# Memory reads of an attention kernel: twelve full-array products, or three blocks of sixteen 32x32 tiles in the score banks

## The chip, the cores and the metric

The kernel runs on one core of a Trainium2 chip. The metric is the device time of one execution in microseconds. Five engines work side by side, each on its own list of instructions in order: PE (TensorE, matmuls; its weight loads are shown as PEld), DVE (VectorE), ACT (ScalarE), POOL (GpSimd) and SP, which here only issues DMAs. They wait for each other through semaphores. Matmuls write PSUM, eight banks of 128 partitions by 512 float32 values; VectorE and ScalarE read the banks.

## The reference, cut to what matters

```python
g = sigmoid((x * gate_w).sum(-1))            # x: 2048 x 448, 16 heads of 28
for s in range(4):                           # segments of 512 rows
    p = softmax(qs @ ks.T * scale + mask); a_dot = p @ vs
    pq = phi(qs)                             # t + 1 if t > 0 else exp(t)
    a_mem = (pq @ M) / (pq @ z + 1e-6)       # M: 28 x 28 and z: 28, for each head
    outs.append(gb * a_mem + (1 - gb) * a_dot)   # gb = sigmoid(beta), one for each head
    M = M + phi(ks).T @ vs;  z = z + phi(ks).sum(0)
a = concat(outs) @ wo
b = (gelu(layernorm(x).T @ w1 + b1) @ w2 + b2).T  # w1: 2048 x 1792, w2: 1792 x 2048
out = g * a + (1 - g) * b
```

In the first segment M and z are zero, so there is nothing to read from the memory.

## The kernel before, in words

The kernel is a list of operations, made once by Python, each with the engine it runs on, what it reads and writes, and a name. `ORDER` (line 286 on) then gives for each engine the order of the names as a fixed list: an engine never runs ahead of its list. Waits follow from what operations read and write. In the PE list `name@4` says that the operation takes PSUM bank 4 (of the four rotating banks 4 to 7), and `u1-3*2` stands for u1-3 and u1-4.

The names that matter:

- `lo…`, `pr…`: projections of x to queries, keys and values (`pair`, line 654). `tk`, `gk`, `gq` are DMAs on SP: transposes of the key features, and a regrouping of the last four heads through DRAM.
- `sc{p}_{f}` (`scores`, line 930): the scores of two units at a time. A unit is one segment and a group of four heads; u = 4 s + group, sixteen in all. One operation fills banks 0 to 3, four row tiles of 28 rows at once (line 942), and `exp{p}_{f}` on ScalarE reads all four banks in one instruction of 128 x 2048 (line 951). There are 40 of them, five for two units, and they share these four banks. Masks (line 954) are GpSimd's.
- `pv{u}` (line 978): probabilities times values, four column strips of 32.
- `mem{u}` (line 965, from unit 4 on): the read of the memory, one product of 512 columns. The four heads' M lie in one 128 x 128 matrix with zeros off the diagonal (`mst_sb`). The result goes to a rotating bank.
- `ta{u}` (line 994) and `tm{u}` (line 992): VectorE's transposing copies of the two results out of PSUM. Then `eps`, `rec`, `oa`, `om`, `o` combine them (lines 1003 to 1011), and `ot{u}` (line 1016) turns the result back.
- `wo{T}` (line 1022): the output projection of a tile of 128 rows; `ag{T}` gates it, on ScalarE or VectorE.
- `mst{s}`, `msta{s}`, `mstc{s}` (line 818 on): update of the memory after a segment, on PE (line 827, 64 small products) and VectorE; `mstc` (line 845) multiplies with a mask `maskg` that holds gb and the zeros off the diagonal.
- `u{ft}-{st}` (`mm1`) and `y{T}-{ft}` (`mm2`): the two layers of the token MLP, 224 and 238 products, most of PE's work. `gsq`, `gvh`, `garg`, `gth`, `gelu` make the gelu of one u tile between ScalarE and VectorE; `fin{T}` (line 1082) makes an output tile, which `out{T}` stores. The last tile, T = 15, is cut in 320 and 128 columns.
- `ldw1_k_p`, `ldw2_k_p` (`ring_load`, line 550): w1 and w2 come in fifteen blocks of four quarters through a ring of three slots. A quarter is loaded again only when the products that read its old content are done.

PE works in forms: full array or column strips (`f`), four row tiles (`r`, the scores), two row tiles (`h`, `lo…`). In a run between two scores or `lo…` that contains a `c` operation (pv, mst), the full products are issued as four column strips (`mm`, line 261), so that the form need not change within the run. Such a product has four records in the profile, all at line 264.

Of the kernel before, what the change touches and what calls it, by code (L numbers as in the profile page):

```python
# [6 lines left out]
ALU = mybir.AluOpType  # L7
# [7 lines left out]
DH = 28  # L15
NSEG = 4
F = 1792
NT = 16
# [56 lines left out]
class Sched:  # L75
# [13 lines left out]
    def op(self, eng, fn, reads=(), writes=(), name=None, dma=False, out=False, cost=100.0, prio=0.0, mode="f",  # L89
# [13 lines left out]
        o.tile = mode if mode in "rh" else "f"  # L103
# [176 lines left out]
def pool_cost(n):  # L280
# [7 lines left out]
warm gtr@4 warm2 pra0@5 pra1@6 pra2@7 pra3@4 prb3 prb2 prb0 prb1 lot2 lot0 prt1 prt3 prt2 prt0 pra0_1 pra0_2 pra0_0  # L288
btr@5 lok0_0 lok0_2 prk0_0 prx0_3 prk0_2 prk0_1 loq1_2@74 loq1_0@65 prq1_2h prq1_1 prq1_2 prq1_0 loq0_0 lok1_0@57
prk1_1 prq0_0 loq0_2 lok1_2@64 prk1_0 prx1_3 prk1_2 prq0_2 prq0_2h prq0_1 lot4@75 lot6@46 prt7 prt6 prt4 prt5 sc0_0  # L290
lok2_2@64 prx2_3 u1-0@7 u0-0@5 u1-1 prk2_2 u1-2 u0-1 u1-3*2 u0-2*4 u1-5 sc0_1 lok2_0@46 prk2_1 u1-6*2 prk2_0
u2-0@6*2 sc0_2 u2-2 u0-6 u2-3 u1-8*2 u0-7 u2-4 u0-8*3 u2-5 sc0_3 u1-10 u0-11*3 u2-6 u0-14 u1-11 u0-15 u2-7*2 u1-12
u2-9 sc0_4 u1-13 u2-10 u1-14 u2-11 u4-0@4*2 u1-15 u4-2 pv0@5 u4-3 sc1_0 u2-12 u4-4 u2-13 u3-0@5*2 u2-14 u4-5 u3-2
u4-6 u3-3*2 u2-15 pv1@7 u3-5*2 u4-7 u3-7 sc1_1 u4-8*2 u3-8 u4-10 u6-0@7 u5-0@6 u4-11 u5-1 u6-1*2 u3-9 u4-12*3 u3-10
u4-15 u3-11 u6-3*3 sc1_2 u3-12*2 u5-2 u6-6*2 u3-14 u7-0@4 u3-15 u6-8*4 u5-3 u7-1 u6-12*4 u7-2 sc1_3 u5-4 u7-3*2
u5-5*3 u8-0@5 u5-8*2 u7-5 u8-1 u5-10*3 u7-6 sc1_4 u8-2 u7-7 u5-13 u8-3 pv2@7 u7-8 u8-4 u5-14 u8-5 u7-9 u5-15 u7-10
sc2_0 u8-6 mst0@7 u8-7*3 u7-11 u8-10 u9-0@6 u8-11 u9-1 sc2_1 u8-12*2 u9-2 u8-14*2 u9-3 pv3@7 u9-4 u7-12*2 u9-5
u7-14 u9-6 u7-15 u9-7 sc2_2 loq2_0@75 u9-8*2 prq2_1 u9-10*2 prq2_0 sc2_3 loq2_2@45 prq2_2 u9-12*2 wo2@7 u9-14
prq2_2h u9-15 sc2_4 mem4@4 wo0#1@7 wo3@5 pv4@6 wo1@4 sc3_0 lot8@75 prt9 u10-0@6*2 prt8 u10-2*2 sc3_1 u10-4*2 mem5@4
pv5@5 u10-6*5 sc3_2 u10-11 u11-0@4 u10-12 u11-1 u10-13*3 mst1@5 u11-2*4 sc3_3 lot10@75 u11-6*3 prt11 u11-9 prt10  # L300
u13-0@6 sc3_4 u11-10*2 mem6@5 u13-1 u11-12 pv6@7 u11-13 u13-2 u12-0@5 u11-14*2 u13-3 sc4_0 u12-1 u13-4*3 u12-2
u13-7*2 mem7@7 u13-9 u12-3*2 u13-10 sc4_1 u12-5 u13-11*2 pv7@4 u13-13*2 u12-6 u13-15 u12-7*3 sc4_2 lok3_0@74
u12-10*3 prk3_0 u12-13*3 prk3_1 sc4_3 lok3_2@67 prx3_3 prk3_2 loq3_0@45 prq3_0 sc4_4 prq3_1 wo6@6 wo7@7 sc5_0 wo5@4
wo4@6 pv8@7 y2-0@5*2 sc5_1 y2-2 y1-0@4 y2-3*2 y1-1 pv9@6 y2-5 y1-2 mem8@7 sc5_2 y1-3 y2-6 y1-4 y0-0@6 y1-5*3 y2-7
y0-1 y1-8 mem9@7 sc5_3 y0-2*3 y1-9 y2-8 y1-10 y0-5 y2-9 y0-6 y4-0@7 y2-10 y1-11 y4-1 y0-7 sc5_4 y2-11*2 y0-8 y2-13
y1-12*2 y4-2 y0-9*3 y5-0@5 y0-12 y5-1 y4-3 sc6_0 y4-4 mem10@4 y5-2 y4-5*2 y5-3 y0-13 y5-4*2 y4-7 y5-6*3 sc6_1 y4-8
pv10@4 y5-9*2 mem11@6 y5-11*3 y4-9 y3-0@4 sc6_2 y4-10 y3-1 y4-11 y3-2 y4-12*2 pv11@6 y3-3*2 sc6_3 lot14@57 y3-5
prt15 y3-6 mst2@6 prt14 y3-7*2 sc6_4 loq3_2@67 prq3_2 y3-9 prq3_2h y6-0@5 y3-10*2 y6-1 y3-12 lot12@67 sc7_0 y3-13
prt12 prt13 y6-2*3 mem12@4 sc7_1 y6-5 wo10@6 y6-6 wo8@4 pv12@7 y8-0@6 y6-7 y8-1*3 wo11@4 y8-4 mem13@7 y6-8 y8-5
sc7_2 y6-9 pv13@4 y7-0@7 y6-10 y8-6*2 y6-11*3 y8-8*2 mem14@4 sc7_3 y8-10 y7-1*2 wo9@5 pv14@4 y7-3 sc7_4 y7-4 y9-0@5  # L310
y8-11*3 y9-1 y7-5 y9-2 y11-0@4 y7-6 y9-3*2 y7-7 y9-5 y7-8 y9-6 y7-9 y9-7 y7-10 y9-8 pv15@6 y11-1 y7-11*2 y9-9*3
mem15@6 y11-2*6 y7-13 y9-12*2 y10-0@6*4 y11-8 y10-4*4 y11-9 y10-8*3 y11-10*4 y10-11*3 wo12@7 wo15@5 wo13@6 wo14@4
y13-0@7*2 y12-0@5 y13-2 y12-1 y15-0@6 y12-2*2 y14-0@4*2 y12-4 y13-3*2 y12-5*3 y14-2*4 y12-8 y13-5 y15-1 y14-6 y15-2
y14-7*3 y13-6*2 y14-10 y15-3*2 y14-11 y15-5*2 y13-8*3 y14-12 y13-11 y12-9 y14-13 y12-10 y15-7 y13-12*2 y15-8 y12-11
y15-0#1@4 y12-12*2 y15-9*5 y15-1#1 y15-2#1 y15-3#1 y15-4#1 y15-5#1 y15-6#1 y15-7#1 y15-8#1 y15-9#1 y15-10#1
y15-11#1 y15-12#1 y15-13#1""",
    "ACT": """
ldwv0 ldgw ldwv1 ldwv2 ldwvb ldwkb ldb1 ldb2 cpv2 cpv0 gt0 gt2 cpv1 gt3 gt1 ek0_0 cpk0_3 cpk0_1 cpq1_1 cpq1_2
cpq1_0 cpq0_3 cpq1_2#1 cpk1_1 eq1_2 eq1_1 ek0_1 cpk1_0 cpk1_3 cpq1_3 cpk1_2 cpq0_2 cpq0_0 cpq0_2#1 cpq0_1 cpv7 cpv6
gt7 cpv4 gt6 cpv5 gt4 gt5 exp0_0@2 cpk2_3 cpq2_3 tb exp0_1@3 eq1_0 cpk2_0 exp0_2@4 ek0_2 exp0_3@0 gsq0 exp0_4@1  # L320
gsq1 gth0 gvh1 exp1_0@5 ek0_3 gsq2 gth1 exp1_1@6 gth2 ek1_0 eq1_3 gsq4 gvh4 exp1_2@2 gth4 gsq3 ek1_1 gsq6 exp1_3@3
ek1_2 gth3 exp1_4@0 gth6 gsq5 exp2_0@1 gth5 ek1_3 exp2_1@4 gsq8 gvh8 gsq7 exp2_2@5 cpq2_1 gth7 exp2_3@6 ag2 gsq9
exp2_4@0 ag0 gth8 exp3_0@2 eq2_0 gt9 exp3_1@3 gth9 gt8 ek2_1 exp3_2@1 gsq10 ek2_0 exp3_3@4 cpv11 cpv10 gt11 gt10
exp3_4@0 eq2_1 gsq11 exp4_0@5 gth10 gth11 exp4_1@6 eq2_2 gsq13 exp4_2@7 cpk3_0 gsq12 gth13 exp4_3@2 cpk3_2 cpq3_3
exp4_4@3 ag6 gth12 exp5_0@0 ag5 exp5_1@1 ek2_2 exp5_2@4 ek2_3 exp5_3@5 eq2_3 exp5_4@6 eq3_0 exp6_0@2 exp6_1@3 eq3_1
exp6_2@7 exp6_3@0 cpv15 gt15 cpv14 gt14 exp6_4@1 exp7_0@4 cpv12 gt12 gt13 eq3_2 ag10 ag8 exp7_1@5 ag11 eq3_3
exp7_2@6 exp7_3@2 ag9 exp7_4@3 ag15 ag14""",
# [39 lines left out]
def build_kernel(nc, X, WQ, WK, WV, WO, BETA, W1, B1, W2, B2, GW, OUT):  # L367
# [842 lines left out]
```

## Time and profile before

| | us |
|---|---|
| timed runs, median of three | 172.67 |
| lowest and highest | 172.38, 173.07 |
| profiled execution, span from the first to the last instruction | 170.6 |
| PE busy in the span | 166.8 |
| VectorE busy | 143.7 |
| ScalarE busy | 128.0 |
| GpSimd busy | 61.5 |

The page gives no time of the profiled execution other than its span; what lies around the span is the difference to the timed runs. How to read the views below: the groups have the line, engine, operation, output and input with shape, the count, then the busy time in us and the mean of one in ns. The slices are 40 equal parts of the span, each digit the busy share in tenths. The chain of work that ended last is followed back from the last instruction, so each of its pieces is what held up the next.

### The profile page before, as it was taken

To read this page: it belongs to the slowest core of one execution; us is meant where nothing else is said; L and a number is where in the kernel's file an instruction comes from. 1 tells how busy PE (TensorE), PEld (TensorE's weight loads), DVE (VectorE), ACT (ScalarE), POOL (GpSimd) and SP (SyncE) were. 2 spreads that over 40 slices of the span, in tenths; PEclk is the share of its full clock that TensorE was granted. 3 is DMA by queue.
4 is the path that set the end of the run, shared out by engine and by line. 5 is a ranking of instruction groups with operands and counts; after the bars stand their busy time and mean duration, and the time that the engine had idled before them with its cause. 6 is when DMAs were issued, how large, how long until landed. Compare 5 with 4: busy or idle time off the path is not lost.

```text
span 170.6 us, 5820 instructions
## 1 busy us (share of the span) xinstructions
PE 166.8 (98%) x2470; PEld 81.3 (48%) x2470; DVE 143.7 (84%) x327; ACT 128.0 (75%) x158; POOL 61.5 (36%) x94
## 2 busy tenths in 40 slices
PE   8899999999999999999999999999999999999994
PEld 2334444455444544545444345444454645555563
DVE  3088998858999899999999989999999999998024
ACT  0359997999999999989999999986897879002100
POOL 5000317255044333229465560446834372500000
DMA  6998994999796816234037286116146251553603
GB/s 145 252 280 274 238 219 138 290 256 183 173 235 168 142 33 184 38 94 138 4 115 207 65 257 112 33 32 187 46 143 200 83 156 50 156 161 112 188 4 108
DMA packets 52589, 25.16 MB, mean 148 GB/s; under 512 B 17092, under 2 KB 52324, under 8 KB 52564
## 3 DMA queue, kind: packets, MB, share of 16 engines
q1 hardware_dynamic: 51772, 24.22, 56.5%
q10 hardware_dynamic: 792, 0.58, 1.7%
q8 instruction: 19, 0.31, 0.8%
q14 instruction: 6, 0.05, 0.1%
HBM read 18.76 MB, written 2.36 MB: 124 GB/s over the span
## 4 chain that ended last, share of the span: by engine, by line
PE 93%; DMA 3%; SPq 2%; DVE 0%; issue 0%
PE t L264 80%; PE t L942 8%; PE t L978 5%; DMA t<-in_A_wk_dram 3%; SPq L521 2%; PE t L827 1%; DVE t L636 0%; DVE t L1082 0%; PE t L860 0%
## 5 line engine op out<-in xcount | busy, mean ns | idle before, releaser
L264 PE MATMUL t<-t 128*32 128x448 bf16 (+6 forms) x1753 | 145.2, 348 | 0.6 <-DMA t<-in_A_wv_dram 0.5
L264 PEld LDWEIGHTS t<-t 128*32 128x32 bf16 (+1 forms) x1753 | 66.8, 97 | 63.3 <-issue 12.8
L951 ACT ACTIVATE t<-t 128x2048 bf16<-128x2048 f32 x40 | 75.1, 1877 | 8.1 <-PE t L942 7.5
L954 POOL TENSOR_SCALAR_AFFINE_SELECT t<-t 128x512 bf16<-128x512 bf16 x64 | 43.4, 694 | 46.4 <-ACT t L951 45.4
L1009 POOL TENSOR_TENSOR t<-t 128x448 bf16<-128x448 f32 x9 | 11.3, 1254 | 18.9 <-DVE t L1007 9.2
L1082 DVE SCALAR_TENSOR_TENSOR t<-t 128x448 bf16<-128x448 f32 (+2 forms) x17 | 10.8, 643 | 8.6 <-PE t L264 8.1
L1036 ACT ACTIVATE t<-t 128x448 bf16<-128x448 f32 x10 | 7.2, 725 | 12.0 <-PE t L264 11.9
L942 PE MATMUL t<-t 28*128 28x512 bf16 (+3 forms) x256 | 15.8, 301 | 0.0
L994 DVE STREAM_TRANSPOSE t<-t 128x512 f32<-128x512 f32 x16 | 11.3, 709 | 1.2 <-PE t L978 0.8
L894 POOL TENSOR_TENSOR t<-t 128x4 f32<-128x4 f32 x4 | 4.3, 1069 | 21.4 <-DVE t L892 16.9
L978 PE MATMUL t<-t 128*32 128x512 bf16 (+3 forms) x256 | 11.5, 299 | 0.0
L942 PEld LDWEIGHTS t<-t 28*128 28x128 bf16 x256 | 4.4, 92 | 14.6 <-ACT t L951 5.9
L1016 DVE STREAM_TRANSPOSE t<-t 128x512 bf16<-128x512 bf16 x16 | 11.0, 689 | 0.1
L885 DVE BATCH_NORM_STATS2 t<-t 128x6 f32<-128x448 bf16 x16 | 9.2, 610 | 0.7 <-DMA t<-in_A_x_dram 0.7
L1060 DVE TENSOR_SCALAR t<-t 128x448 f32<-128x448 f32 x11 | 7.3, 671 | 2.7 <-ACT t L1054 2.7
L1067 DVE SCALAR_TENSOR_TENSOR t<-t 128x448 bf16<-128x448 f32 x14 | 8.7, 622 | 1.0 <-ACT t L1065 1.0
L978 PEld LDWEIGHTS t<-t 128*32 128x32 bf16 x256 | 6.9, 97 | 5.0 <-DVE t L992 0.2
L1054 ACT ACTIVATE t<-t 128x448 f32<-128x448 f32 x14 | 8.9, 636 | 0.3 <-PE t L264 0.2
L1005 DVE SCALAR_TENSOR_TENSOR t<-t 128x448 f32<-128x448 f32 x12 | 9.0, 750 | 0.1
L1062 DVE SCALAR_TENSOR_TENSOR t<-t 128x448 f32<-128x448 f32 x14 | 8.8, 629 | 0.3 <-ACT t L1057 0.2
L750 ACT ACTIVATE t<-t 128x512 bf16<-128x512 bf16 x12 | 7.5, 629 | 1.5 <-DVE t L707 1.5
L992 DVE STREAM_TRANSPOSE t<-t 128x512 f32<-128x512 f32 x12 | 8.4, 704 | 0.2
(71 smaller groups left out, 132.6 us busy)
## 6 DMA issues: line engine op xcount, KB each, us to landing
t<-in_B_w_dram SPq DMA_DIRECT2D x52, 256.0 KB, 3.8
t<-in_A_x_dram SPq DMA_DIRECT2D x4, 448.0 KB, 4.7
out_dram<-t SPq DMA_DIRECT2D x15, 112.0 KB, 2.6
t<-in_B_w_dram SPq DMA_DIRECT2D x8, 128.0 KB, 3.6
t<-in_A_wv_dram ACTq DMA_DIRECT2D x4, 112.0 KB, 4.2
t<-in_A_wo_dram SPq DMA_DIRECT2D x4, 98.0 KB
t<-in_A_wq_dram SPq DMA_DIRECT2D x1, 336.0 KB, 4.8
spare_heads<-t SPq DMA_DIRECT2D x8, 32.0 KB
```

Of the source, the lines that this page charges most:

```text
L264: last = e.matmul(out[q], w[:, q], x, skip_group_check=True, **kw)
L885: op("DVE", lambda e: e.bn_stats(st6[:, t, :], xh[:, t, :]), reads=[R_x[t]], writes=[R_st6[t]], name=f"bns{t}", cost=512, prio=P_PROJ - 10 ...
L942: last = e.matmul(bank(hl)[:, c0 : c0 + w], kT[r, hg, s * 512 + j * 128 : s * 512 + j * 128 + 128], qT[r, hg, s * 512 + 128 * j : s * 512 ...
L951: op("ACT", lambda e: e.activation(pslot(g), ps[:, 0:4, :], ACT.Exp, scale=SCALE), reads=R_bank[0:4], writes=[g.res], take=g, name=f"exp{p ...
L954: op("POOL", lambda e, c0=c0: e.affine_select(pslot(g)[:, :, c0 : c0 + 128], pslot(g)[:, :, c0 : c0 + 128], pattern=[[0, 4], [1, 128]], co ...
L978: last = e.matmul(bank(cb)[32 * hl : 32 * hl + 32, 128 * j : 512], vaug[:, 4 * s + j, 32 * h : 32 * h + 32], pslot(P_fill[u // 2][f])[:, h ...
L994: dv(lambda e: e.transpose(t2[:, 0, :], bank(cb)[:, 0:512]), [bres(cb)], [R_tt[tb][0]], "ta", 630, use=(cb,))
L1005: dv(lambda e: e.scalar_tensor_tensor(n3[0], n3[0], oc, rb[0], op0=ALU.mult, op1=ALU.mult), [R_tt[tb][0], R_rec[tb], R_omcol], [R_tt[tb][0 ...
L1009: op("POOL", lambda e: e.tensor_tensor(o3, n3[0], n3[1], op=ALU.add), reads=R_tt[tb], writes=[R_ob[tb]], name=f"o{u}", cost=1280, port=Tru ...
L1016: dv(lambda e: e.transpose(oT[:, hg, s * 512 : s * 512 + 512], o), [R_ob[tb]], qres(hg, s), "ot", 635)
L1054: op("ACT", lambda e: e.activation(gg[:, q, :], bank(b)[:, 0:D], ACT.Square, bias=b1s[:, ft : ft + 1], scale=math.sqrt(GC)), **buse(b), re ...
L1082: op("DVE", lambda e: e.scalar_tensor_tensor(outst[:, p, c0:c1], bank(b)[:, 0 : c1 - c0], omg[:, T : T + 1], ag(T)[:, c0:c1], op0=ALU.mult ...
```

## The change

The twelve `mem{u}` go. For each of the segments 1 to 3 one operation `mem{s}` computes the reads of all four units, as sixteen matmuls of 32 x 32 tiles with 512 columns each: head strip hl of group hg is read by row tile hl and goes to column strip (hl + hg) % 4 of bank hg. It writes the score banks 0 to 3, is a form of its own (`q`), and stands in the order between two scores of the middle of the segment's attention. The four `tm` of a segment follow it. They write four buffers kept for the segment (`tt` grows from four to six).

For the tiles to fall so, the heads of a group are rotated: `pv` writes the strip (hl + hg) % 4 too, and the rows of WO are loaded in the rotated order, by seven DMAs instead of four. The memory is kept as 32 columns for each group without the zeros (`mst_sb`), so `mstc` multiplies 128 columns instead of 512, and the mask is made in small steps.

All five orders are new: the same work is laid out anew between the scores. On PE the last output tile's two parts come earlier, and y13, with 448 columns, is last. VectorE and ScalarE exchange some of the readings of banks that either may do. SP's ring loads, gathers and stores stand in another order.

The core of the diff:

```diff
     def load_wo():
-        for hl in range(4):
-            op("SP", lambda e, hl=hl: e.dma_start(wo_sb[32 * hl : 32 * hl + DH, :, :],
-                                                  WO.rearrange("(g l d) m -> l d g m", g=NHG, l=4)[hl]),
+        for q in range(4):
+            for k, (g0, g1, h0) in enumerate(((0, q + 1, q), (q + 1, NHG, 4 * q + 7))[: 2 if q < 3 else 1]):
+                rows = WO.rearrange("(h d) m -> h d m", d=DH)[h0 : h0 + 3 * (g1 - g0 - 1) + 1 : 3]
+                op("SP", lambda e, q=q, g0=g0, g1=g1, rows=rows: e.dma_start(
+                    wo_sb[32 * q : 32 * q + DH, g0:g1, :], rows.rearrange("g d m -> d g m")),
...
-        op("DVE", lambda e: e.tensor_tensor(mst_sb[:, s].rearrange("p g (l c) -> p g l c", l=4),
-                                            mst_f32[:, :, None, :].to_broadcast([128, NHG, 4, 32]), maskg[:, :, :, :],
-                                            op=ALU.mult),
+        op("DVE", lambda e: e.tensor_tensor(mst_sb[:, s], mst_f32[:], maskg[:], op=ALU.mult),
...
-        mb, cb = Bank(), Bank()
-        if s > 0:
-            op("PE", lambda e, cols=False: mm(e, bank(mb)[:, 0:512], mst_sb[:, s - 1, hg, :],
-                                              phq[:, hg, (s - 1) * 512 : s * 512], cols, start=True, stop=True),
-               reads=[R_mst[s - 1]] + [R_phq[hg][s], P_fill[u // 2][1 + 3 * (u % 2)].res], writes=[bres(mb)], take=mb, name=f"mem{u}", mode="x",
-               cost=pe_cost(512), prio=pr)
+        cb = Bank()
...
-                    last = e.matmul(bank(cb)[32 * hl : 32 * hl + 32, 128 * j : 512],
+                    last = e.matmul(bank(cb)[32 * ((hl + hg) % 4) : 32 * ((hl + hg) % 4) + 32, 128 * j : 512],
...
+    def mem_four(s):
+        mbs = list(range(NHG))
+        pr = P_ATT + 4 * s
+
+        def fn(e):
+            for hg in range(NHG):
+                for hl in range(4):
+                    r = slice(32 * hl, 32 * hl + 32)
+                    c = 32 * ((hl + hg) % 4)
+                    last = e.matmul(bank(mbs[hg])[c : c + 32, 0:512], mst_sb[r, s - 1, hg, :],
+                                    phq[r, hg, (s - 1) * 512 : s * 512], start=True, stop=True, skip_group_check=True)
+            return last
+
+        op("PE", fn, reads=[R_mst[s - 1]] + [R_phq[hg][s] for hg in range(NHG)], writes=R_bank[0:4],
+           name=f"mem{s}", mode="q", cost=512 / 2.4 + 20, prio=pr)
+        for hg in range(NHG):
+            u, b, t = 4 * s + hg, mbs[hg], tt[:, 2 + hg, :]
+            op("DVE", lambda e, b=b, t=t: e.transpose(t, bank(b)[:, 0:512]), reads=[bres(b)], writes=[R_tt[2 + hg]],
+               name=f"tm{u}", cost=630, prio=pr)
```

The new order around the blocks and at the end, PE:

```
... sc2_2 loq2_0@45 prq2_1 prq2_0 u8-8*3 mem1 loq2_2@54 u8-11*3 prq2_2 u8-14*2 u9-7 prq2_2h u11-0@5*2 u9-8 u11-2*3 sc2_3 ...
... sc4_2 prq3_1 wo3@4 wo2@6 mem2 y0-0@5*4 y1-0@6*3 y0-4*4 y1-3*2 y0-8 sc4_3 ...
... sc6_2 lot12@67 y4-0@4*2 prt13 y4-2 prt12 mem3 y6-8 y4-3 y6-9 y4-4*3 lot14@67 prt15 prt14 sc6_3 ...
... y14-3*3 wo13@5 y13-0@6*3 y14-6*2 y13-3 y12-7 y13-4*3 y12-8*5 y14-8*6 y12-13 y13-7*7
```

and VectorE before and in the copies of the first and second block:

```
... gelu6 phq1_0 mk1_3 cpq2_1 phk1_3 tm5 tm7 cpq2_2 rec2 tm6 tm4 eps4 ...
... gelu12 rec7 om7 gelu13 oa7 tm10 tm8 tm9 tm11 cpq3_3 ot7 ...
```

SP, around the load that the prediction follows: `... ldw2_3_0 tk2_3 gk3_2 out0 gq3_h1 gq3_h2 gk3_h0 ldw2_3_1 ldw2_3_3 gk3_h1 tk2_2 gq3_h0 out2 ldw2_3_2 ldw2_4_2 ldw2_5_0 ...`, and at the end `... ldw2_7_2 ldw2_7_3 ldw2_6_1 out10 out11 ldw2_6_2 out15 out9 out15#1 out14 out12 out13`.

More of the change, by code (lines that the diff above doesn't have):

```diff
@@ L102, in op @@
         o.mode = mode
-        o.tile = mode if mode in "rh" else "f"
+        o.tile = mode if mode in "rhq" else "f"
         o.cols = False
@@ L298 @@
[L298 to L307, printed above, removed]
@@ new lines @@
+u4-12 u5-1*2 u4-13*3 u5-3 u6-1 u5-4*2 u6-2 u5-6 pv1@6 sc1_3 u5-7*4 u6-3*9 sc1_4 u5-11 u6-12*4 u7-0@5*3 u5-12*4
+u7-3*2 u8-0@6 u7-5*2 sc2_0 u7-7*7 mst0@4 u8-1*3 sc2_1 u8-4*2 pv2@4 u7-14*2 u9-0@7*7 u8-6*2 sc2_2 loq2_0@45 prq2_1
+prq2_0 u8-8*3 mem1 loq2_2@54 u8-11*3 prq2_2 u8-14*2 u9-7 prq2_2h u11-0@5*2 u9-8 u11-2*3 sc2_3 u9-9*4 pv3@4 u11-5*2
+u10-0@6*2 u9-13*3 sc2_4 u11-7*3 u10-2 u12-0@4*3 u10-3 pv4@7 u12-3 u11-10*3 sc3_0 u11-13*3 u10-4*2 u13-0@7 u10-6*5
+u12-4 sc3_1 u10-11*2 u13-1*2 u12-5 u10-13*3 pv5@5 u12-6 u13-3*2 u12-7*4 sc3_2 lot8@56 u13-5*2 u12-11*2 prt8 prt9
@@ new lines @@
+u12-13*2 sc3_3 u13-7*3 u12-15 u13-10 wo0#1@6 u13-11*4 mst1@5 u13-15 sc3_4 lok3_0@64 prk3_0 prk3_1 pv6@5 sc4_0
+lot10@76 prt10 prt11 pv7@4 wo1@5 sc4_1 lok3_2@67 prk3_2 loq3_0@45 prq3_0 prx3_3 sc4_2 prq3_1 wo3@4 wo2@6 mem2
+y0-0@5*4 y1-0@6*3 y0-4*4 y1-3*2 y0-8 sc4_3 loq3_2@47 y1-5*6 prq3_2 y1-11*2 sc4_4 y0-9 y1-13 y0-10*4 pv8@4 prq3_2h
+sc5_0 y3-0@6*7 y2-0@7*3 y3-7 sc5_1 y2-3 wo5@5 y3-8*6 y2-4 sc5_2 y5-0@4*2 y2-5 pv9@5 wo4@6 y2-6 sc5_3 y5-2 y2-7 wo6@5
+y2-8 wo7@6 sc5_4 y5-3*2 y2-9*3 y5-5*3 pv10@5 sc6_0 y5-8*3 y6-0@5 y2-12*2 y5-11*2 pv11@6 sc6_1 y5-13 y6-1*7 mst2@4
@@ L489, in build_kernel @@
     R_vh, R_gg = R("vh", 2), R("gg", 2)
-    R_tt = [R(f"tt{i}_", 2) for i in range(2)]
+    R_tt = R("tt", 6)
     R_rec = R("rec", 2)
@@ L844, in do_mst @@
                writes=[R_mstf], name=f"msta{s}", cost=dve_cost(128), prio=P_BASE)
[L845 to L848 removed]
+        op("DVE", lambda e: e.tensor_tensor(mst_sb[:, s], mst_f32[:], maskg[:], op=ALU.mult),
+           reads=[R_mstf, R_maskg], writes=[R_mst[s]], name=f"mstc{s}", cost=dve_cost(128), port=True, prio=P_BASE)
     def do_small():
@@ L985, in pv_unit @@
            cost=564, prio=pr)
-        t2 = tt[:, tb]
+        ia, im = tb, 2 + hg
+        t2 = tt[:, ia : im + 1 : im - ia, :] if s > 0 else tt[:, ia : ia + 1, :]
         def dv(fn, reads, writes, name, cost, **kw):
             op("DVE", fn, reads=reads, writes=writes, name=f"{name}{u}", cost=cost, prio=pr, **kw)
-        if s > 0:
-            dv(lambda e: e.transpose(t2[:, 1, :], bank(mb)[:, 0:512]), [bres(mb)], [R_tt[tb][1]], "tm", 630,
-               use=(mb,))
-        dv(lambda e: e.transpose(t2[:, 0, :], bank(cb)[:, 0:512]), [bres(cb)], [R_tt[tb][0]], "ta", 630, use=(cb,))
-        t3 = [t2[:, k, :].rearrange("p (b c) -> p b c", c=32) for k in range(2)]
+        dv(lambda e: e.transpose(tt[:, ia, :], bank(cb)[:, 0:512]), [bres(cb)], [R_tt[ia]], "ta", 630, use=(cb,))
+        t3 = [tt[:, k, :].rearrange("p (b c) -> p b c", c=32) for k in (ia, im)]
         dens = t2.rearrange("p k (b c) -> p k b c", c=32)[:, :, :, DH]
@@ L1086, in mm2 @@
         op("SP", lambda e: e.dma_start(out2[T * 128 : T * 128 + 128, c0:c1], outst[:, p, c0:c1]),
-           reads=[R_outst[4 if c0 else p]], name=f"out{T}", dma=True, out=True, cost=500, nbytes=256 * (c1 - c0))
+           reads=[R_outst[4 if c0 else p]] + ([R_outst[4]] if T == NT - 5 else []), name=f"out{T}", dma=True, out=True, cost=500, nbytes=256 * (c1 - c0))
     def mm2_last(T):
@@ L1146, in build_kernel @@
             scores(u // 2, f)
+        if u % 4 == 0 and u > 0:
+            mem_four(u // 4)
         pv_unit(u)
```

178 lines of the change are left out of this document (89 added, 89 removed).

## The prediction

> **What bounds the kernel now.** I read the page first: the share of busy time, the slices and the chain that ended last.
>
> ```profile
> span 170.6 us, 5820 instructions
> PE 166.8 (98%) x2470; PEld 81.3 (48%) x2470; DVE 143.7 (84%) x327; ACT 128.0 (75%) x158; POOL 61.5 (36%) x94
> PE   8899999999999999999999999999999999999994
> DVE  3088998858999899999999989999999999998024
> PE 93%; DMA 3%; SPq 2%; DVE 0%; issue 0%
> ```
>
> TensorE is busy in every slice and 93% of the chain is its own. "Busy" can hide stalls, so the next view is the busy time by windows: one over the stretch after the start-up, then three of its parts.
>
> ```profile
> 9.05:168.25 159.20, 159.17 (x2442) 78.58 (x2442) 141.32 (x321) 126.46 (x157) 59.07 (x79) 1.00 0.58 145
> 40.00:80.00 40.00, 40.00 (x678) 20.07 (x674) 37.95 (x79) 38.91 (x45) 14.18 (x21) 1.00 0.61 144
> 120.00:148.00 28.00, 28.00 (x581) 14.78 (x573) 27.18 (x54) 21.57 (x23) 14.03 (x20) 1.00 0.38 113
> ```
>
> Columns are the length, then PE, PEld, DVE, ACT, POOL, the granted clock, DMA. PE is busy 159.17 of 159.20 us at a clock of 1.00; VectorE is at 95 to 97% and ScalarE at 97% in places. The third view, the chain in order of time (start, length, what), tells whether PE issues without pauses, because its pieces can be compared with the order written in the kernel:
>
> ```profile
> 57.84 0.49 PE t L827 x64
> ...
> 118.28 0.33 PE t L942 x8
> 118.61 0.30 PE t L264 x4
> 118.92 0.54 PE t L978 x16
> 119.46 1.54 PE t L264 x32
> 121.00 0.33 PE t L942 x8
> ...
> 143.29 3.90 PE t L264 x80
> ...
> 168.27 0.35 DVE t L1082
> ```
>
> L264 is the helper of all full-array products (a product split into four column strips has four records), L942 the scores, L978 the probabilities times values, L827 the memory update. After the last score the order has twenty products of 448 columns, 80 records: 3.90 us. A score is followed by one such product in 0.30 us. If p is a product and w the change of tile form after a score, 20p + w = 3.90 and p + w = 0.30: p = 0.189, w = 0.11. The piece at 119.46 is eight operations of which one is a memory read (mem11): 1.54 - 7 x 0.189 = 0.217 us for a read of 512 columns. So PE runs gap-free from 9 us on, and **the time is the sum of PE's instructions plus its changes of tile form**. There is no idle time to win: only less PE work makes it faster, and any new wait of PE adds in full.
>
> **The change, part by part.** *Memory reads.* Twelve reads at 0.217 us go: -2.60. Three blocks of sixteen 32x32 tiles come. The trace has none; the nearest row is the score, whose four row tiles of 512 columns, each filling a bank of its own, take 0.33 us with the change of form into it, and 0.11 to get out: 0.44. Sixteen tiles have twelve more instructions to issue; the memory update issues 64 in 0.49 us, 7.7 ns each, so 0.09 more: 0.53 a block, **+1.59**. Bounds: 0.44 if issuing hides (+1.32 in all); above, if only four of the sixteen run at a time, three more passes of 0.22 (0.33 less 0.11), 0.66 a block, +2.0 over my value.
>
> *Changes of form.* I counted them in both PE orders: 105 before, 112 after. Six of the seven more belong to the blocks and are in the 0.53; one is left: +0.1. Everything else in the two PE lists has the same columns, and up to the first projections the same order, so the start to 9 us stays. PE: -2.60 + 1.59 + 0.1 = **-0.9**.
>
> *The end.* Before, the last product is the 128-column part of the last output tile; after, it is a full tile of 448 (y13).
>
> ```profile
> L1082 DVE SCALAR_TENSOR_TENSOR t<-t 128x448 bf16<-128x448 f32 x15 | 9.9, 668 | 8.5 <-PE t L264 7.9 <-DMA out_dram<-t 0.5
> L1082 DVE SCALAR_TENSOR_TENSOR t<-t 128x128 bf16<-128x128 f32 x1 | 0.4, 351 | 0.2 <-PE t L264 0.2
> out_dram<-t SPq DMA_DIRECT2D x3, 112.0 KB, 1.7
> out_dram<-t SPq DMA_DIRECT2D x1, 32.0 KB, 1.5
> ```
>
> The groups by form and the transfers of the last 6 us say: VectorE's last step 0.67 instead of 0.35, the landing 1.7 instead of 1.5. Both stand behind PE: **+0.5**.
>
> *The new wait.* A block writes score banks 0 to 3. It must follow the ScalarE exp of the score before, and the next score must follow VectorE's four transposing copies (tm) of the whole segment. Behind that score on PE stands everything, as PE issues in order. Before, a read took one rotating bank and nobody's score waited. The rows for the distances:
>
> ```profile
> 120.93 0.40 PE L942 MATMUL t<-t 28*128 28x256 bf16 x8
> 123.43 0.39 PE L942 MATMUL t<-t 28*128 28x512 bf16 x4
> 121.38 1.88 ACT L951 ACTIVATE t<-t 128x2048 bf16<-128x2048 f32 x1 [0.32 <-PE t L942]
> 149.13 0.72 DVE L992 STREAM_TRANSPOSE t<-t 128x512 f32<-128x512 f32 x1
> 149.77 0.67 DVE L1016 STREAM_TRANSPOSE t<-t 128x512 bf16<-128x512 bf16 x1
> ```
>
> From a score's first matmul to its reader 0.45 (120.93 to 121.38); from the reader's end to the next score 0.17 (121.38 + 1.88 to 123.43), the smallest gap I find, 2.50 from score to score; a copy starts 0.64 after the one before and lasts 0.72. So after a block the next score can come at the earliest 0.45 + 0.09 + 3 x 0.64 + 0.72 + 0.17 = 3.35 us after the block's first matmul, with VectorE free. The order gives PE between mem2 and the score sc4_3 fourteen products: 0.22 + 0.09 + 0.11 + 14 x 0.189 + 0.11 = 3.18. PE waits 0.17. The other two blocks have about the same filling (six products, a pair and two value projections behind mem3; twelve products, a pair and two query projections behind mem1, with two short VectorE instructions between the copies): **+0.5** for three. Lower bound 0 if VectorE hands back sooner than ScalarE; above, VectorE's own lateness, a rival below.
>
> *Other tight places.* From score to score the new order has several stretches of eleven products, 11 x 0.189 + 0.33 + 0.11 = 2.52, at the 2.50 that the exp needs, and a few a shade shorter: **+0.1**.
>
> *What costs nothing, and under what cover.* VectorE's three masking multiplies shrink, and seven of its readings of banks go to ScalarE net:
>
> ```profile
> L845 DVE TENSOR_TENSOR t<-t 128x512 bf16<-128x512 f32 x3 | 2.0, 681 | 0.0
> L840 DVE COPY t<-t 128x128 f32<-128x128 f32 x1 | 0.3, 282 | 0.0
> L873 DVE TENSOR_TENSOR t<-t 128x448 f32<-128x448 bf16 x1 | 0.6, 621 | 0.0
> L1005 DVE SCALAR_TENSOR_TENSOR t<-t 128x448 f32<-128x448 f32 x12 | 9.0, 750 | 0.1
> L1004 DVE RECIPROCAL t<-t 128x32 f32<-128x32 f32 x12 | 4.0, 336 | 0.1
> 149.55 0.47 SPq L1086 DMA_DIRECT2D out_dram<-t  x1
> t<-in_B_w_dram SPq DMA_DIRECT2D x10, 256.0 KB, 3.8
> ```
>
> The multiply on 128 instead of 512 columns goes from 0.68 to about 0.28; the mask's one 0.62 becomes small instructions. Four gatings, two halvings and one key copy, 0.67 each by the nearest row (the output step), leave VectorE: some 6 us less in all, and some 4 us more on ScalarE (estimates). PE covers both while they keep up; a copy of a bank that is late costs PE its lateness. On POOL two of the additions change place, and its masks too, 36% busy. On SP three more loads of WO go out among ring loads; WO is first read at wo0, some 84 us in. The ring of w1 and w2 is fed by the same in-order queue. I followed it by the order: the quarters refilled with least room are the last of w2's block 7 (5.5 us of PE work between the last use of the old and the first of the new, 3.8 to land) and quarter 2 of block 3, which stands behind the store of tile 2. That store waits for pv10, its copy (0.72), a reciprocal (0.34), a scaling (0.75) and the output step (0.67): with PE's 0.54, two issues of 0.47 and 3.8 to land, 7.8 us, where PE has 8.3 by the prices above between pv10 and y6-8. Cover of 0.5; beyond that each us costs one.
>
> **The sum.** -0.9 + 0.5 + 0.5 + 0.1 = +0.2 on the profiled span of 170.6. That span is 2.1 below the median of the timed runs, 172.67 (172.38 to 173.07), which I take as what lies around it and unchanged: 172.87, **172.9**.
>
> The Trainium skill, TensorEngine Tiling (Array Packing), section Theoretical Speedup, gives up to 16x when both dimensions are at most 32. By that a block is one pass, as I take it; no trace here shows it for both dimensions.
>
> **The rivals.**
>
> *The gain comes whole (172.0).* VectorE's copies do not hold PE and issuing hides: -2.60 + 1.32 + 0.1 + 0.5 = -0.7. For it: each of the three waits is only 0.17 by my rows. It is also the floor: PE has 0.03 us idle to give back.
>
> *The four copies come late (slower, 174.9).* Place: VectorE ahead of tm5, tm10 and tm13. If one more instruction of 0.62 to 0.75 us stands before the first copy when the block ends, all four copies and the next score, and so PE, are that much later; three times 0.65 is +2.0 over the forecast. It decides from the point where VectorE reaches the first copy over 0.5 us after the block's first matmul. For it: VectorE is 95 to 97% busy in the windows, and the copies of four units now fall due at once. Against: VectorE's list is the 6 us shorter. The Trainium skill says the same of the mechanism (TensorEngine Tiling (Array Packing), section PSUM Bottleneck: tiling speeds TensorE but not the emptying of PSUM); the windows agree so far as they show VectorE at 27.18 of 28.00.
>
> *The sixteen tiles do not run together (slower, 174.9).* Each bank gets its four head strips from four row tiles at once, in different partitions; in the scores each row tile has a bank to itself. If row tiles took turns on a bank, four passes would be needed: +0.66 a block, +2.0. For it: no row shows that sharing. Against: column strips (L978) share a bank at full speed, 0.54 us for sixteen. In the Trainium skill, Gotcha 1 under Restrictions and Gotchas of TensorEngine Tiling (Array Packing) speaks for it: different row tiles cannot use one PSUM bank at a time. No trace here shows the rule tested with separate partitions.
>
> *A ring quarter lands late (173.9).* Landing 1.5 us over the 3.8 at y6-8 uses up the 0.5: +1.0.
>
> **How the numbers follow.** Forecast 0.43, whole gain 0.16, late copies 0.26, tiles in turn 0.10, ring 0.05. The bound of 0.5%, about what a measurement of this kernel can tell from no change, is 171.8 to 173.5. The forecast lies within it; of the whole gain I put 0.06 below 171.8, by the spread of the runs, and 0.10 within. Faster 0.06, same 0.53, slower 0.41. The range takes in the floor with the spread and the dearer cases: 171.8 to 174.9; that of the likeliest case alone is 172.3 to 173.5.
>
> **What would show it.** PE's chain: the three blocks as x16 pieces of about 0.4 us; four times that means tiles in turn. PE idle before sc2_3, sc4_3 and sc6_3, released by the VectorE copy: about 0.2 each is my forecast, none the whole gain, 0.7 and more the late copies. PE's last matmul near 0.3 us earlier than 168.25; the last step 0.67 and a landing of 1.7. PE waits released by in_B_w transfers mean the ring. My prediction is wrong if PE has idle stretches elsewhere, for then the new order, not the tiles, sets the time.

## The result and the profile after

The changed kernel takes **173.68 us** (median of 13 runs, 173.38 to 174.25), the kernel before 172.73 beside it (13 runs, 172.12 to 173.49): the ratio is 1.0056, 95% interval 1.0038 to 1.0074. That is slower by 0.95 us, just over the half per cent, where 0.2 was forecast. The profiled spans say the same, 170.6 to 171.7. Where the 1.1 us between them comes from can be read from four views. First the page, its busy times, slices and chain:

```profile
span 171.7 us, 5711 instructions
PE 165.6 (96%) x2415; PEld 79.7 (46%) x2419; DVE 140.2 (82%) x322; ACT 132.5 (77%) x165; POOL 60.6 (35%) x94
PE   8799999999999999999999999999999999999992
PE 85%; DVE 5%; SPq 5%; DMA 3%; issue 1%
```

PE is busy 1.2 us less than before and yet the kernel is slower; 5% of the chain now belongs to VectorE, where it was 0%. The windows place it (columns as before: length, then PE, PEld, DVE, ACT, POOL, clock, DMA):

```profile
9.00:168.57 159.57, 158.29 (x2387) 77.12 (x2391) 137.47 (x316) 130.97 (x164) 58.35 (x79) 1.00 0.59 144
40.00:80.00 40.00, 39.76 (x633) 19.74 (x626) 37.73 (x85) 38.45 (x47) 11.61 (x17) 1.00 0.68 151
80.00:120.00 40.00, 39.56 (x585) 18.48 (x577) 37.85 (x78) 38.28 (x45) 21.00 (x27) 1.00 0.50 108
```

The first row sums up the middle: PE's busy time fell from 159.17 to 158.29, by 0.88, and its idle time rose from 0.03 to 1.28. The second and third rows hold 0.24 and 0.44 us of it; before, the same stretches had none. The chain in order of time shows the blocks (L1018), three of the waits and the end:

```profile
18.13 0.61 DVE t L719
...
18.78 2.83 PE t L264 x14
...
64.28 0.36 PE t L1018 x16
...
66.85 1.29 PE t L264 x6
...
99.30 0.46 PE t L1018 x16
99.75 0.02 issue
99.78 2.51 DVE t L1026 x4
102.28 0.59 DVE t L719
102.87 0.05 issue
102.92 2.23 PE t L264 x13
...
127.82 0.40 PE t L1018 x16
...
168.59 0.68 DVE t L1096
```

L1026 is the transposing copy of a score bank, L719 a copy of a projection out of its bank. At 99.78 the chain leaves PE for VectorE: four copies, 2.51 us, and behind them the copy cpq3_3, after which PE may write the bank. In the timeline of the same place PE's score comes before that and is hardly delayed:

```profile
99.78 2.51 DVE L1026 STREAM_TRANSPOSE t<-t 128x512 f32<-128x512 f32 x4 [0.18 <-PE t L1018]
102.21 0.65 DVE L719 CAST t<-t 128x512 bf16<-128x512 f32 x1
102.35 0.39 PE L942 MATMUL t<-t 28*128 28x512 bf16 x4
102.92 0.58 PE L264 MATMUL t<-t 64*128 64x256 bf16 x3 [0.17 <-DVE t L719]
```

The score sc4_3 starts at 102.35, some 0.06 after the copies end (99.78 + 2.51). The half-K remainder of a query projection, loq3_2, starts at 102.92 only. To find all such places I set the start of every PE operation beside the time it would have if it followed the one ahead without a pause (0.189 us a product of 448 columns, about 0.1 a change of form). From 18 us on the order has these delays in us:

```
lot6    0.40   VectorE's copy cpq1_3, behind layer-norm statistics
u11-0   0.25   VectorE's copy cpq2_2, behind two of the first block's four copies
loq3_2  0.24   VectorE's copy cpq3_3, behind the second block's four copies
lok3_0  0.18   a bank or operand whose readers end at 87.7 to 87.8
pv15    0.11   a mask on POOL
y6-0, y10-0, wo15   0.09, 0.08, 0.08   a transposition on VectorE
lok2_0  0.06   a bank that isn't free yet
```

They are 1.49 together, 0.49 behind the copies and 1.0 elsewhere; with the start of the three blocks' followers (0.04 each) 1.6. This count is 0.2 to 0.3 above the idle time of the window because the record of the last matmul reaches, as busy time, into the start of a wait: at lot6 the timeline shows 0.23 idle for the 0.40. PE's last matmul ends at 168.57 instead of 168.25 in the windows' bounds: +0.32. After it come 171.7 - 168.57 = 3.1 us, where before it was 170.6 - 168.25 = 2.35: +0.8. The two make the 1.1.

### The profile page after: what moved, and what is told of

Read it like the earlier page. It is cut to its first block, busy times and chain, and to the rows that moved or that the text cites. A ratio compares the mean times of both kernels' runs of the same rounds, so it can differ in the third digit from the quotient of the medians.

```text
span 171.7 us, 5711 instructions
## 1 busy us (share of the span) xinstructions
PE 165.6 (96%) x2415; PEld 79.7 (46%) x2419; DVE 140.2 (82%) x322; ACT 132.5 (77%) x165; POOL 60.6 (35%) x94
## 4 chain that ended last, share of the span: by engine, by line
PE 85%; DVE 5%; SPq 5%; DMA 3%; issue 1%
PE t L264 71%; PE t L942 7%; PE t L972 5%; SPq L516 4%; DMA t<-in_A_x_dram 3%; DVE t L885 2%; DVE t L1026 1%; PE t L825 1%; SPq L506 1%; PE t L1018 1%; DVE t L719 1%; DVE t L1096 0%; DVE t L752 0%; SPq L510 0%; DVE t L763 0%
## 5 line engine op out<-in xcount | busy, mean ns | idle before, releaser
L264 PE MATMUL t<-t 128*32 128x448 bf16 (+8 forms) x1650 | 141.7, 347 | 2.1 <-DMA t<-in_A_wv_dram 0.8
L264 PEld LDWEIGHTS t<-t 128*32 128x32 bf16 (+2 forms) x1654 | 64.8, 97 | 64.7 <-issue 14.1
L1050 ACT ACTIVATE t<-t 128x448 bf16<-128x448 f32 x14 | 10.1, 725 | 13.4 <-DVE t L911 7.6
L1096 DVE SCALAR_TENSOR_TENSOR t<-t 128x448 bf16<-128x448 f32 (+2 forms) x17 | 10.7, 644 | 9.2 <-PE t L264 9.2
L1000 POOL TENSOR_TENSOR t<-t 128x448 bf16<-128x448 f32 x9 | 10.7, 1184 | 14.9 <-DVE t L998 8.3
L986 DVE STREAM_TRANSPOSE t<-t 128x512 f32<-128x512 f32 x16 | 11.4, 713 | 3.8 <-PE t L972 3.8
L787 ACT ACTIVATE t<-t 128x448 bf16<-128x448 f32 x12 | 6.4, 546 | 4.5 <-PE t L264 4.5
L885 DVE BATCH_NORM_STATS2 t<-t 128x6 f32<-128x448 bf16 x16 | 9.2, 608 | 0.8 <-DMA t<-in_A_x_dram 0.8
L1076 DVE SCALAR_TENSOR_TENSOR t<-t 128x448 f32<-128x448 f32 x14 | 9.6, 684 | 0.2
L996 DVE SCALAR_TENSOR_TENSOR t<-t 128x448 f32<-128x448 f32 x12 | 8.9, 739 | 0.1
L752 DVE SCALAR_TENSOR_TENSOR t<-t 128x512 bf16<-128x512 bf16 x12 | 8.4, 703 | 0.1
## 6 DMA issues: line engine op xcount, KB each, us to landing
t<-in_B_w_dram SPq DMA_DIRECT2D x8, 128.0 KB, 3.7
```

The costliest lines, as they stand in the source:

```text
L264: last = e.matmul(out[q], w[:, q], x, skip_group_check=True, **kw)
L885: op("DVE", lambda e: e.bn_stats(st6[:, t, :], xh[:, t, :]), reads=[R_x[t]], writes=[R_st6[t]], name=f"bns{t}", cost=512, prio=P_PROJ - 10 ...
L986: dv(lambda e: e.transpose(tt[:, ia, :], bank(cb)[:, 0:512]), [bres(cb)], [R_tt[ia]], "ta", 630, use=(cb,))
L1000: op("POOL", lambda e: e.tensor_tensor(o3, n3[0], n3[1], op=ALU.add), reads=[R_tt[ia], R_tt[im]], writes=[R_ob[tb]], name=f"o{u}", cost=12 ...
L1050: op("ACT", lambda e: e.activation(ag(T), bank(b)[:, 0:D], ACT.Identity, bias=b2g[:, T : T + 1], scale=gcol[:, T : T + 1]), **buse(b), rea ...
L1076: op("DVE", lambda e: e.scalar_tensor_tensor(gg[:, q, :], gg[:, q, :], 1.0, vh[:, q, :], op0=ALU.add, op1=ALU.mult), reads=[R_gg[q], R_vh[ ...
```

## The experiments

**Theory A:** the tiles do save what they should, and three separate things take it back: waits behind the four copies in a row, other waits that the new lists brought, and a longer end after PE. The edits below try to take each away by itself. **Rival B:** VectorE (with ScalarE) paces the kernel, so that PE's waits are only its symptoms: take one away and it comes back elsewhere.

**The ending alone.** The 128-column remainder of token tile 15, its add and its store come last, as before the change:

```diff
-PE ... wo15 y15-0*5 y15-0#1 y15-5*2 y15-1#1 ... y15-13#1 y12-5 ... y12-13 y13-7*7
+PE ... wo15 y15-0*10 wo14 y15-10*4 wo12 ... y14-8*6 y13-7*7 y15-0#1 y15-1#1 ... y15-13#1
-DVE fin15#1 fin15 fin14 fin12 fin13      SP out15 out9 out15#1 out14 out12 out13
+DVE fin15 fin12 fin14 fin13 fin15#1      SP out15 out9 out12 out14 out13 out15#1
```

> The changed kernel, with only its end put in another order: the 128-column part of the last output tile is again the last product, and its output step and store are last too. Theory A (the loss is PE waits that the new lists make, plus a longer end): the last output step 0.35 instead of 0.67, the landing 1.5 instead of 1.7, fewer waits of SP behind it: 0.6 to 0.8 us faster than the changed kernel, so about 172.95. Rival B (VectorE is the bound now, PE's waits and the end are only where that shows): 0.0 to 0.2 faster.

It took 173.46 us, 1.0052 (1.0030 to 1.0074) of before: on the medians almost the changed kernel, though its profiled span was 171.1 instead of 171.7. So the changed kernel was run again by itself:

> The changed kernel once more, unaltered, beside the kernel before on the same chip, so that the next three have a partner of the same hour. Both theories: 173.4 to 174.0 us, 1.004 to 1.007 of before. If it comes out under 1.003, the short gain that the trace of the altered ending showed would be lost in the scatter; if near 1.0056, that kernel's 1.0052 says that the 0.55 us of its one profiled span was mostly not a gain.

The control took 173.85 us, 1.0068 (1.0050 to 1.0087). And the altered ending once more:

> The kernel with the altered ending again (the 128-column remainder of the last token product, its add and its store come last), in one session with the next two. Theory A (the end after TensorE costs what the two traces show): 0.4 to 0.6 us under the changed kernel, 1.002 to 1.003 of before. Rival B (the store lands when its queue lets it, whatever comes last): 0.2 us or less under it, 1.005 or more.

This time 173.17 us, 1.0031 (1.0013 to 1.0049), 0.68 under the control. By the ratios, each taken beside the kernel before, the two pairs give 0.1 and 0.6 us, and a third pair, below, 0.9; the first alone would fit B. The traces are steadier than the medians: from PE's last matmul to the end of the span it is 3.1 us in every kernel with the new ending (171.7 - 168.57 here; 172.1 - 169.03 in the control) and 2.3 to 2.6 with the altered one (171.5 - 169.16 in the second). The chain of that run ends with the short step (the edits shift the lines a little: L1093 here is L1096 of the changed kernel):

```profile
169.18 0.35 DVE t L1093
```

So A holds for the ending, at about 0.6. The scatter is elsewhere, in two places. Of the profiled runs, the first half-K remainder of a key projection starts at 10.26 us in one and 10.88 in another, and all that follows moves with it. And the waits themselves differ between executions of one kernel: from that remainder to PE's last matmul the changed kernel took 158.21 us, the control, the same program, 158.72. In the control's trace lot6 waits 0.26 instead of 0.40, the third memory update takes 0.2 longer, and the score sc1_3 waits about 0.3 for its exp:

```profile
46.99 1.87 ACT L951 ACTIVATE t<-t 128x2048 bf16<-128x2048 f32 x1
...
48.91 0.39 PE L942 MATMUL t<-t 28*128 28x512 bf16 x4 [0.23 <-ACT t L951]
```

So neither a single span nor a single stretch of PE tells anything under half a microsecond.

**Copies of projections moved ahead (three misses).** In the first, cpq3_3 goes ahead of the second block's copies on VectorE, and four products of unit 9 ahead of u11-0 on PE:

```diff
-DVE gelu13 oa7 tm10 tm8 tm9 tm11 cpq3_3 ot7       PE prq2_2h u11-0*2 u9-8 u11-2*3 sc2_3 u9-9*4 pv3
+DVE gelu13 oa7 cpq3_3 tm10 tm8 tm9 tm11 ot7       PE prq2_2h u9-8*4 u11-0*2 sc2_3 u11-2*3 u9-12 pv3
```

> The changed kernel, with two edits at the memory blocks only: on VectorE the key-query copy cpq3_3 stands ahead of the four copies of the second block instead of behind them, and on PE four products of u9 come before the first two of u11 behind the first block. Theory A: the waits of PE for a bank whose reader stands behind the four copies (0.25 at u11-0, 0.24 at loq3_2) go: 0.4 to 0.5 us faster than the changed kernel, about 173.2. Rival B: the waits come back at the next score or bank, 0.0 to 0.1 faster.

175.34 us, 1.0152 (1.0123 to 1.0182), 1.5 above the control. Its timeline says why:

```profile
100.71 0.43 PE L1018 MATMUL t<-t 32*32 32x512 bf16 x16
...
102.06 0.69 DVE L719 CAST t<-t 128x512 bf16<-128x512 f32 x1 [0.99 <-ACT t L717]
...
102.67 2.50 DVE L1026 STREAM_TRANSPOSE t<-t 128x512 f32<-128x512 f32 x4
...
105.22 0.40 PE L942 MATMUL t<-t 28*128 28x512 bf16 x4 [1.33 <-DVE t L1026]
```

cpq3_3 reads the bank that ScalarE's cpk3_3 (L717) reads too, and is released by it: VectorE stands idle for 0.99 us, the copies begin 1.96 us after the block's first matmul (100.71 to 102.67) instead of 0.55 (99.23 to 99.78), and the score behind them waits 1.4. In its place behind the copies cpq3_3 had cost PE 0.24. And u11-0's 0.25 reappeared at once before the score sc2_3. The new wait is 1.2 more than the old one; this trace, of the longest of the six executions, also has sc1_3 waiting 0.7 for its exp, ahead of both edits.

The second moves two early copies ahead of the statistics, and a halving ahead of a feature map of queries:

```diff
-DVE mq1_1 bna0 bns10 vpe0 cpq1_2#1 cpq1_3 bns4     gelu11 phq2_2 gvh12 garg12
+DVE mq1_1 cpq1_2#1 cpq1_3 bna0 bns10 vpe0 bns4     gelu11 gvh12 phq2_2 garg12
```

> The changed kernel, with two edits on VectorE away from the blocks: the copies cpq1_2#1 and cpq1_3 come before a layer-norm statistic instead of behind it, and gvh12 before phq2_2. Theory A: PE's wait of 0.40 at lot6 and of 0.18 at lok3_0 go: 0.4 to 0.6 us faster than the changed kernel, about 173.15. Rival B: 0.0 to 0.1 faster.

174.23 us, 1.0094 (1.0072 to 1.0116). The wait of lot6 is 0.26 instead of 0.40, but it is 0.26 in the unaltered control too, so the edit is not shown to have shortened it; lok3_0 keeps its 0.18. The chain now runs, behind the copy, through the layer norm on VectorE for 5 us:

```profile
17.88 0.69 DVE t L719
...
19.24 2.63 DVE t L885 x5
...
24.94 3.52 PE t L264 x16
```

The statistics (L885) are late instead, and with them what stands behind on VectorE and ScalarE; lok2_0 waits 0.58 where it had waited 0.06.

> The changed kernel with the edits of the end, of the blocks and of the two places away from the blocks together. Theory A: the parts add, 1.4 to 1.9 us faster than the changed kernel, 171.8 to 172.3, which is 0.4 to 0.9 faster than the kernel before. Rival B: 0.0 to 0.4 faster than the changed kernel, 173.3 or more.

With all three edits 174.62 us, 1.0116 (1.0094 to 1.0139): both new waits are there (1.40 and 0.58), and the shorter ending. On where the waits can be mended A was wrong: the lists are tight, and a copy moved forward pushes back another that PE needs as soon.

**What the tiles are worth.** Four whole products at each block's place:

```diff
-for hl in range(4): e.matmul(bank(mbs[hg])[c : c + 32, 0:512], mst_sb[r, s - 1, hg, :], phq[r, hg, ...])
+e.matmul(bank(mbs[hg])[:, 0:512], vaug[:, 4 * (s - 1), 128 * hg : 128 * hg + 128], phq[:, hg, ...])
```

> The same lists, places and banks, but each block is four whole 128x128 products in place of sixteen 32x32 tiles; the products read a piece of the value table as weights, so this kernel leaves out the true memory read and its output is another. Theory A (the tiles run four at a time, and TensorE's work plus the waits in its list set the time): a block takes 4 x 0.217 = 0.87 us and no change of form around it, where the tiled one takes 0.36 to 0.46 and about 0.1 for the changes, so 0.40 to 0.50 more a block and 1.2 to 1.5 us over the kernel changed, 174.8 to 175.2 us. Rival B (VectorE and ScalarE set the pace and TensorE's list only waits for them): the longer blocks eat into the waits behind them (0.25 before a position product of unit 11, 0.24 before the remainder of a query projection of segment 3), so under 0.9 us over the changed kernel.

174.66 us, 1.0123 (1.0102 to 1.0143), 0.8 above the control. The rows of its blocks (L1015), from the chain:

```profile
64.21 0.86 PE t L1015 x4
...
99.48 0.88 PE t L1015 x4
```

0.87 against 0.36 to 0.46. From the product ahead to the product behind, with the changes of form, a block is 0.40 to 0.50 longer, 1.4 for three; one of the waits behind (u11-0) vanished, which gave 0.25 back, as B said of such waits. The 0.8 by the medians lies in B's range. From the first remainder on, PE needs 159.39 us (10.26 to 169.65) against 158.21 in the changed kernel and 158.72 in the control. So the tiles are worth 0.7 to 1.2 us in this order, on the chip and not only in the count: the saving is real.

**What the copies cost.** Each copy moves 32 of 512 columns:

```diff
-e.transpose(t, bank(b)[:, 0:512])
+e.transpose(t[:, 0:32], bank(b)[:, 0:32])
```

> Each of the twelve VectorE copies of a score bank moves 32 of its 512 columns, so it takes about 0.1 us in place of 0.6 to 0.7; the other columns stay at a zero written once at the start, so the kernel leaves out fifteen sixteenths of the memory term and its output is another. Lists as in the changed kernel. Theory A (the four copies in a row hold back the bank readers behind them, and so TensorE): the waits of 0.25 before the position product of unit 11 and of 0.24 before the remainder of the query projection of segment 3 go, the other five stay, and the time falls by 0.4 to 0.6 us to 173.1 to 173.3. Rival B (VectorE's whole load paces the kernel): 6 us less work on it moves the later waits too, and the time falls by 1.0 us or more.

173.46 us, 1.0046 (1.0026 to 1.0066), 0.4 under the control; one copy took 188 ns instead of 679. The chain at the second block (L1022; the score is L946):

```profile
99.34 0.36 PE t L1022 x16
99.71 2.75 PE t L264 x14
102.47 0.33 PE t L946 x4
102.79 2.16 PE t L264 x13
```

and the window from 98 to 106 us of this kernel:

```profile
98.00:106.00 8.00, 8.00 (x83) 3.69 (x84) 7.13 (x20) 7.31 (x10) 4.14 (x6) 1.00 0.12 28
```

against that of the changed kernel:

```profile
98.00:106.00 8.00, 7.83 (x78) 3.57 (x80) 7.79 (x18) 7.07 (x10) 4.13 (x6) 1.00 0.11 28
```

PE is gap-free there. Exactly two delays are gone, u11-0 and loq3_2; lot6, lok3_0, y6-0, y10-0, pv15, wo15 and lok2_0 keep theirs (0.33, 0.18, 0.09, 0.08, 0.11, 0.08, 0.06). So the four copies cost 0.49 by the trace and 0.4 by the medians. From the first remainder on VectorE is busy 132.53 us instead of 136.23, and yet no other wait behind the blocks moved: VectorE's load as a whole isn't the bound, so B in its strong form falls.

**Copies light and ending altered.** The two edits above together; this kernel, too, leaves out most of the memory term:

> Copies of 32 columns and the altered ending together; it leaves out fifteen sixteenths of the memory term, as the light kernel did. Theory A (the waits behind the four copies and the ending add up): 0.5 and 0.5 off the changed kernel, so 172.6 to 172.9 us, within 1.003 of before, and the five waits that neither touches still there. Rival B (what one gives, the other takes): not under 173.2.

172.56 us, **0.9996 (0.9982 to 1.0011)** of before. The parts add: with these two the loss is gone, to a tenth of a microsecond. Against the altered ending alone (173.17, run beside it) the light copies give 0.6. What is left is a saving of about 1 us in the tiles against waits elsewhere, 0.85 by this kernel's trace; no run takes those away. The pair with and without the altered ending is 0.9 apart here.

**Covering the waits from PE's side.** Work that is ready goes ahead of the product that waits:

```diff
-prq0_1 lot4 lot6 prq0_0 prt7   ...  prq2_2h u11-0*2 u9-8 u11-2*3 sc2_3 u9-9*4 pv3   ...  sc4_3 loq3_2 y1-5*6
+prq0_1 prq0_0 lot4 lot6 prt7   ...  prq2_2h u9-8*5 u11-0*5 sc2_3 pv3               ...  sc4_3 y1-5*2 loq3_2 y1-7*4
```

> Only TensorE's list is altered at three waits, with work that is ready ahead of the waiting product: one whole query projection ahead of the remainders of tokens' projections 4 to 7; two products of unit 1 ahead of the remainder of the segment-3 query projection (one more change of form); five products of unit 9 ahead of the position products of unit 11; and the ending as in the kernel with the altered tail. Theory A (the waits are a matter of TensorE's order alone): 0.40 + 0.24 - 0.1 + 0.25 = about 0.8 us off TensorE's end, and 172.6 to 173.0 us. Rival B (VectorE and ScalarE bring the next operand no sooner): the covered waits come back at the next product that needs a copy, under 0.3 us off TensorE's end, 173.3 or more.

173.27 us, 1.0035 (1.0014 to 1.0055), with the altered ending in it; that ending alone gave 1.0052 and 1.0031, so the covers brought nothing that the runs can tell. The three delays are gone in its trace, but new ones stand behind: lok2_0 0.19 and u0-9 0.11, lok3_0 0.31 instead of 0.18, two of 0.06 to 0.07. Of the 0.89 that went, 0.5 came back and 0.1 is the change of form: PE's stretch is 157.91 us (10.66 to 168.57) against 158.21, so 0.3 shorter where A had 0.8. Beside the control's 158.72 it would be 0.8: the stretches alone can't decide, and the reading rests on the count of the waits and on the medians. Without the first cover:

> All columns copied; the two waits behind the copies covered by other products and the ending altered, the remainder of tokens' projections 4 to 7 left where it was. Theory A (covers at these two places hold, the third only moved its wait): the same as the kernel with three covers or up to 0.1 us more, 173.2 to 173.5 us, since that third cover gave 0.4 and had 0.3 taken back; still 0.5 us above before. Rival B (the third cover was the one that paid): 173.6 or more.

173.44 us, 1.0042 (1.0028 to 1.0056): the same within the intervals, as A expected, no better than the altered ending alone, run beside it (173.17), and again lok3_0 at 0.31. For the waits away from the copies B is nearer: at lok3_0, in both traces, PE waits for what other engines hand over, and comes there earlier to wait longer.

## Why the prediction was right and where it failed

The time fell within the range, 0.8 above the forecast and just past the 173.5 at which the prediction let "slower" begin (it had given that side 0.41). That the range held is in part luck: its upper end stood for late copies and for tiles in turn, and what came in their place were waits to which it had given almost no price. By its own steps:

| step | forecast, us | the runs |
| --- | --- | --- |
| PE's reads, blocks, forms | -0.9 | -0.88 by busy time; +0.32 of the end less 1.5 of waits, about -1.2, by the count |
| waits for the four copies | +0.5 | +0.49 in the trace, 0.4 and 0.6 by the light copies |
| other tight places | +0.1 | +1.0 in the trace |
| after PE's last matmul | +0.5 | +0.8 in the trace; altering the end gave 0.1 to 0.9 in three pairs |
| sum | +0.2 | +1.1 on the span, +0.95 on the medians |

**The tiles** were right in kind and a little dear: 0.53 forecast; in the timeline the next product starts 0.37 after a block's first matmul (64.21 to 64.58, and likewise in the other two), some 0.47 with the change of form ahead of it. That is 0.04 above a score, so the twelve extra instructions cost half of what I gave them. The rival of tiles that take turns in a bank falls: four passes would have shown a row near 1 us (an estimate from the prediction's rows, 0.33 and three more of 0.22). The Trainium skill, TensorEngine Tiling (Array Packing), is answered in both places: its "up to 16x" in Theoretical Speedup agrees with one pass of 0.37 us for sixteen tiles, and where Gotcha 1 under Restrictions and Gotchas has different row tiles unable to use one PSUM bank at a time, the measurement decides against it for tiles that write different partitions.

**The copies** were right in size by chance, and wrong in place. I had PE wait 0.17 before each of three scores, taking the distance from an exp's end to the next score in the trace of before. But PE was never waiting there, so the 0.17 was only the time at which PE came. Where a score does wait for an exp, as in the control above, it is 0.05 us (46.99 + 1.87 to 48.91), and from the end of the copies to the next score it was 0.06, 0.06 and 0.11: no score was late. What was late was the reader of another bank queued among or behind the copies on VectorE, and the product that needs that bank. The rival of late copies half came: by the timeline,

```profile
64.21 0.43 PE L1018 MATMUL t<-t 32*32 32x512 bf16 x16
64.23 0.93 DVE L752 SCALAR_TENSOR_TENSOR t<-t 128x512 bf16<-128x512 bf16 x1
64.58 2.62 PE L264 MATMUL t<-t 64*128 64x256 bf16 x15
65.09 1.30 DVE L1026 STREAM_TRANSPOSE t<-t 128x512 f32<-128x512 f32 x2
```

the first block's copies began at 65.09, 0.88 after its first matmul, behind a feature map of 0.93, and so beyond the point of 0.5 that I had named. But it was paid as the 0.25 of u11-0, not as 0.65. At the second block VectorE was free 0.18 us before the block's banks were ready.

**Other tight places** is the step that failed: +0.1 for stretches from score to score, where not one score waited for an exp in this trace (one did in the control's, about 0.3). The order before had idle time of 0.03 us; I took a new order to be as dense because its VectorE list is lighter (it is, by 3.5 us where some 6 were forecast: 143.7 to 140.2 us busy, while ScalarE rose from 128.0 to 132.5). It is not: 1.0 us of delays stand at seven places that have nothing to do with the blocks, the largest, lot6, before the first score. The prediction's last sign of being wrong, PE idle elsewhere so that the new order sets the time, named this case without giving it a price, and it came: the account of the time was wrong there, though the time was in the range. That the delays are there is shown, and the trace of before has none of them. That they can be ordered away is not shown: the reorderings aimed at two of the seven, lot6 and lok3_0, and moved the wait or made another.

**The end** was under-sized. The step of 0.67 and the landing of 1.7 came as forecast, 0.5 together; the rest is the end of the queue. The last store's landing is followed by about 0.2 us more than before, in which SyncE takes the final waits one after another. That last part is read from the trace only; no run takes it alone.

**The ring and the free edits** cost nothing that shows: PE has no delay at y6-8 beyond the 0.04 behind a block.

## What to carry to other kernels

When a change needs a new order on every engine, the order has a price of its own: find it from the idle time of the bounding engine before and after, not from how much work moved. Copies that fall due together hold back whatever stands behind them on their engine, so ask which bank the next reader there frees and who writes it next. And an engine's list may have no slack even where the engine is busy for only 82% of the time: here five attempts to mend waits of 0.2 to 0.4 us by another order brought nothing measurable or a loss of up to 1.5. And a distance read where the engine was not waiting is no price of a wait: it only bounds it from above.

## What was unexpected of the hardware

Sixteen 32x32 tiles of 512 columns, four row tiles at once in the same bank but in different partitions, take 0.37 us to the next product, 0.04 more than a score whose four row tiles have a bank each (0.33). From the end of VectorE's copies to the first matmul of a score that takes their banks it is only 0.06 us (102.29 to 102.35), and behind ScalarE's exp, where the score had to wait for it, 0.05 (48.86 to 48.91).
